# An mLSTM layer and a mixture of experts on one core: routing of units 16 to 19, the second expert's w2, the last logits and the q/k loads are moved or reshaped

## The chip, the cores and the metric

The kernel runs on one NeuronCore of a Trainium2 chip. The metric is the device time of one execution in microseconds. Engines are named as in the profile: PE (matmul), PEld (its weight loads), DVE (vector), ACT (scalar), POOL (GpSimd), SP (the engine that issues most DMAs).

## The reference

An mLSTM recurrence over 4 batches, 8 heads, 768 tokens with head width 40 gives x (3072 tokens of 320 numbers). A two-level mixture of experts works on x: 4 groups of 4 experts, a hidden width of 1024, the best group and in it the best expert for each token.

```python
m_new = np.maximum(f_gate[:, :, t] + m, i_gate[:, :, t])
f_stab = np.exp(f_gate[:, :, t] + m - m_new)
i_stab = np.exp(i_gate[:, :, t] - m_new)
C = f_stab[:, :, None, None] * C + i_stab[:, :, None, None] * np.einsum('bhd,bhe->bhde', vt, kt)
n = f_stab[:, :, None] * n + i_stab[:, :, None] * kt
denom = np.maximum(np.abs(nq), 1.0)
y[:, :, t] = o * h_tilde / denom
...
g_idx = np.argmax(x @ w_group, axis=1)
e_idx = np.argmax(x[mask_g] @ w_expert[g], axis=1)
h = np.maximum(xg[mask_e] @ w1[g, e], 0.0)
out[tok_idx] = combined[:, None] * (h @ w2[g, e])
```

`combined` is the product of the two softmax weights of the chosen group and expert.

## The kernel before, in words

**Attention.** The recurrence is computed in 6 chunks of 128 tokens. A chunk of one batch is a *unit*, u = 4 c + b, so there are 24. `unit(u)` writes one step of a software pipeline in which neighbours overlap: `scores` (`sp`, L204) of u, `norm1`, `rows`, `rows2` (x, L298) and `store` of u - 1, `mask` (POOL's AFFINE_SELECT, L158) of u + 1, `carried` (`it`, L229), `values` (`av`, L276), `state` (L248), `decay` (`aw` on PE, then four exponentials `ab` on ACT, L187) of u + 2, and `turn` (`tp`, `xT`) of u - 1. q and k lie transposed in a `qk` tile, the heads of r = 0 from partition 0, those of r = 1 from partition 64, 40 rows each; `load_qk` (L140) fills each half with its own DMA of 48 rows (8 of them padding). `store` writes x to DRAM (`x_d`).

**Routing.** For chunks 0 to 4, `logits_of(c)` multiplies the four `xT` tiles of a chunk with the gate weights, ACT copies the result to `lT` (L357), and `logits_back(c)` turns it back (L360) and appends `route` (L365) to `chores`. `route` is a chain of DVE steps (mx, df, eq, m, oh), ranks on PE (L399 to L408), and DVE again (cntf, pr, slf, slot). `go_on(n, slot)` hands out the next steps: "B" steps on DVE at the end of a unit, "A" the ranks on PE. `put_id` (L481) then writes the 128 token numbers of a unit into the table `itab` by an indirect DMA of POOL: four puts a chunk. The last chunk is routed as units 20 to 22 and unit 23 by `logits(u)` (`lg`, L342).

**Order.** Up to unit 21 the instructions stand in the order in which the code writes them; from unit 22 on a scheduler places them, apart from edges that `issue_after` adds.

**Experts.** At unit 14 `first_experts` picks the two experts with the most tokens so far. Their weights are loaded early, half a matrix at a time, by the list `early_loads`: one a unit in units 14 to 19 (w1 of the first, its w2, w1 of the second), the rest, the second's w2, at unit 22. `split_tasks` cuts them into high and low parts (ACT `w1h`, `w2h`, `wsk`; DVE `w1l`, `w2l`, L640). The first expert begins with 256 rows whose tokens are all of chunks 0 to 4: `load_ix` (L611) reads their numbers from `itab`, `load_x` (L578) gathers the rows in two `xg` tiles, `turn_tasks` turns them on PE (`tpm`, L306), and `expert` multiplies with w1 (`psh`, L747) and w2 (`po`). `busy(n)` are matmuls without a reader.

Two `issue_after` edges at the end of the main function (L1005 to L1007) tie the two `tpm` blocks: the first behind `lg` of unit 22, the second behind `tp` of unit 23.

## Time and profile before

| | us |
|---|---|
| three timed runs, median (lowest, highest) | 415.28 (415.12, 416.69) |
| the profiled execution | 414.25 |
| its span | 412.6 |
| PE busy in the span | 386.7 (94%) |
| DVE, ACT, POOL busy | 262.6, 213.7, 167.8 |

The profile is of one execution; all rows below belong to it. A timeline row gives the start from the beginning of the span, the busy time and, in brackets, the engine's idle time before it with what ended that.

### The profile page before, as it was taken

What the parts mean: (1) busy time and instruction counts of PE and PEld (TensorE: products, weight loads), DVE (VectorE), ACT (ScalarE), POOL (GpSimd) and SP (SyncE); (2) the same over time, 40 slices, a digit from 0 to 9 for tenths busy, and PEclk for the clock granted to TensorE, in tenths of its full rate; (3) what the DMA queues carried; (4) which work ended last, traced back from release to release, by engine and by line L of the source; (5) the groups of instructions that cost most, each with busy time, mean ns of one, the idle gap of its engine ahead of it and who ended that gap; (6) DMA issues with size and microseconds to landing.
All of it is one profiled execution on the core that took longest, in us unless ns stands there. A gap on an engine that the chain in (4) does not pass through costs nothing.

```text
span 412.6 us, 9857 instructions
## 1 busy us (share of the span) xinstructions
PE 386.7 (94%) x3665; PEld 361.5 (88%) x3665; DVE 262.6 (64%) x692; ACT 213.7 (52%) x541; POOL 167.8 (41%) x226
## 2 busy tenths in 40 slices
PE   8869999999998985599999999999999999999994
PEld 4769899998887874399999999999999999999994
DVE  5596876868789775385875664765745655433530
ACT  4754555555556611353855564755745645443520
POOL 3235576675664351345805234342032324322300
PEclk9998999999999988579999999999999999999999
DMA  7985789996899981147897557666753267877700
GB/s 201 243 267 151 221 103 222 268 211 136 237 260 240 230 234 42 41 152 239 277 408 250 165 195 256 240 224 185 290 220 136 65 244 258 295 290 262 251 17 11
DMA packets 29029, 84.97 MB, mean 206 GB/s; under 512 B 11831, under 2 KB 15790, under 8 KB 25396
## 3 DMA queue, kind: packets, MB, share of 16 engines
q1 hardware_dynamic: 23812, 67.63, 56.6%
q0 software_dynamic: 4944, 16.34, 11.6%
q8 instruction: 29, 0.48, 0.5%
q10 hardware_dynamic: 224, 0.35, 0.4%
q14 instruction: 20, 0.16, 0.2%
HBM read 74.55 MB, written 9.99 MB: 205 GB/s over the span
## 4 chain that ended last, share of the span: by engine, by line
PE 70%; DMA 12%; issue 9%; POOL 3%; DVE 3%; POOLq 1%; ACT 1%; SPq 0%; DVEq 0%
PE psh L747 14%; PE av L276 7%; PE po L769 6%; PE po L768 6%; PE po L770 6%; PE psh L715 6%; PE sp L204 4%; DMA w2s<-in_w_dram 3%; PE it L229 3%; PE tpm L306 3%; PE aw L177 2%; DMA itab<-tokid,slot 2%; PE it L248 2%; DMA nt<-in_nat_dram 2%; PE po L774 2%
## 5 line engine op out<-in xcount | busy, mean ns | idle before, releaser
L187 ACT ACTIVATE ab<-aw,bcol 128x128 f32<-128x128 f32 x192 | 54.5, 370 | 50.1 <-PE aw L177 49.7
L582 POOL DMA_INDIRECT out_dram<-y,ix x32 | 37.8, 1181 | 82.8 <-ACT y L780 68.8
L768 PE MATMUL po<-w2h,hh 128*128 128x320 f32 (+3 forms) x200 | 63.1, 316 | 0.0
L770 PE MATMUL po<-w2h,hh 128*128 128x320 f32 (+3 forms) x200 | 61.8, 309 | 0.0
L769 PE MATMUL po<-w2l,hh 128*128 128x320 f32 (+3 forms) x200 | 61.8, 309 | 0.0
L640 DVE TENSOR_TENSOR w2l<-w2s,w2h 128x640 fp32r<-128x640 f32 x64 | 50.6, 815 | 10.6 <-ACT w2h L638 10.6
L578 POOL DMA_INDIRECT xg<-x_d,ix x32 | 35.3, 1102 | 53.8 <-DMA ix<-itab 33.0
L276 PE MATMUL av<-nt,pt 128*128 128x128 f32 x384 | 50.1, 285 | 0.1
L276 PEld LDWEIGHTS av<-nt,pt 128*128 128x128 f32 x384 | 47.6, 201 | 0.9 <-DVE pt L209 0.3
L704 DVE SCALAR_TENSOR_TENSOR hh<-psh,hh 128x256 fp32r<-128x256 f32 (+4 forms) x108 | 36.0, 366 | 18.0 <-ACT hh L701 17.5
L701 ACT ACTIVATE hh<-psh 128x288 fp32r<-128x288 f32 (+8 forms) x68 | 30.1, 443 | 30.1 <-PE psh L747 15.4
L638 ACT CAST w2h<-w2s 128x640 fp32r<-128x640 f32 x64 | 43.2, 724 | 0.4 <-DMA w2s<-in_w_dram 0.4
L715 PE MATMUL psh<-xhl,w1s 128*128 128x144 f32 (+3 forms) x336 | 41.3, 283 | 0.0
L715 PEld LDWEIGHTS psh<-xhl,w1s 128*128 128x128 f32 x336 | 40.9, 191 | 0.1
L780 ACT ACTIVATE y<-po,xg 128x320 f32<-128x320 f32 (+3 forms) x25 | 13.2, 527 | 52.1 <-PE po L770 49.7
L747 PE MATMUL psh<-xhl,w1h 128*128 128x256 f32 (+5 forms) x224 | 38.6, 295 | 0.9 <-DVE xhl L683 0.5
L209 DVE TENSOR_TENSOR pt<-sp,ab 128x512 f32<-128x512 f32 x48 | 31.0, 685 | 10.2 <-PE sp L204 9.3
L769 PEld LDWEIGHTS po<-w2l,hh 128*128 128x128 f32 (+3 forms) x200 | 36.5, 183 | 0.0
L768 PEld LDWEIGHTS po<-w2h,hh 128*128 128x128 f32 (+3 forms) x200 | 36.5, 182 | 0.0
L770 PEld LDWEIGHTS po<-w2h,hh 128*128 128x128 f32 (+3 forms) x200 | 36.4, 182 | 0.0
L747 PEld LDWEIGHTS psh<-xhl,w1h 128*128 128x128 f32 x224 | 32.5, 196 | 1.5 <-DVE xhl L683 0.8
L204 PE MATMUL sp<-qk 40*128 40x128 f32 x384 | 29.5, 286 | 1.3 <-DVE pt L209 1.3
(193 smaller groups left out, 772.4 us busy)
## 6 DMA issues: line engine op xcount, KB each, us to landing
w1s<-in_w_dram SPq DMA_DIRECT2D x12, 1536.0 KB, 6.9
w2s<-in_w_dram SPq DMA_DIRECT2D x12, 1280.0 KB, 7.9
qk<-in_qkT_dram SPq DMA_DIRECT2D x48, 192.0 KB, 6.7
nt<-in_nat_dram SPq DMA_DIRECT2D x24, 324.0 KB, 6.3
x_d<-x SPq DMA_DIRECT2D x24, 192.0 KB, 7.1
sig<-in_og_dram SPq DMA_DIRECT2D x6, 640.0 KB, 7.1
w1s<-in_w_dram SPq DMA_DIRECT2D x4, 768.0 KB, 10.9
w1s<-in_w_dram POOLq DMA_DIRECT2D x2, 1536.0 KB, 7.1
```

Source lines behind the costliest of these rows:

```text
L187: rt["exp"] = nc.scalar.activation(st_[u]["ab"][:, r, j, :], aw[:, j, :], AF.Exp, bias=bcol[:, c, i:i + 1])
L204: mm(t["pm"][r][:, pr, :], qk[rs, 0, pr, :], qk[rs, 1, pr, :], start=True, stop=True)
L276: ins = mm(av[:, i:i + P], t["pm"][r][:, pr, :], nt[:, o:o + P], start=True, stop=True)
L582: return nc.gpsimd.indirect_dma_start(out=out, out_offset=bass.IndirectOffsetOnAxis(ap=idx, axis=0), in_=y, in_offset=None, bounds_check=N ...
L638: nc.scalar.copy(a, src[:, s])
L640: lows.append(lambda: nc.vector.tensor_tensor(o[rows], src[rows, s], a[rows].bitcast(F32), op=ALU.subtract))
L704: nc.vector.scalar_tensor_tensor(hh[:, f:f + per, dst], src[:, :, t], 0.0, hr.bitcast(F32)[:, :, t], op0=ALU.max, op1=ALU.subtract)
L715: ins = mm(ps[:, g * W:(g + 1) * W], w1s[:, s], xhl[:, k, :], start=(k == 0), stop=(k == 2))
L747: ins = mm(ps[:, g * W:(g + 1) * W], w[:, s], x, start=(n == 0), stop=(n == len(todo) - 1))
L768: mm(po[0:m], hh[:, f, t], w2h[:, s], start=st0, stop=False)
L769: mm(po[0:m], hh[:, f, t], w2l[:, s], start=False, stop=False)
L770: ins = mm(po[0:m], hh[:, f, tl], w2h[:, s], start=False, stop=sp0)
```

## The change

- `load_qk` is one DMA of 80 rows, into partitions 24 to 103 of the `qk` tile. r = 0 now contracts rows 0 to 63, the first 24 of which are zeros that POOL writes once; r = 1 contracts rows 64 to 103 as before. `kw` gets the same places, with POOL's zeros between.
- `logits_of(c)` stands ahead of the second `decay` of its unit, `logits_back(c)` at the end of the same unit (before: in the next unit).
- In unit 21, `route` of chunk 4 is written in the middle of the unit: four "B" steps ahead of `rows2`, the ranks, three "B" steps, and all four `put_id` there.
- The two halves of the second expert's w2 are issued by POOL instead of SP; POOL also loads that expert's number into a register for it.
- Both `tpm` blocks of the first expert are tied behind `lg` of unit 23.

```diff
+Z = 64 - D
+KS = 64 + D
-    kws = [ap_.tile([P, H * D + 24], F32, name=f"kw{i}") for i in range(2)]
+    kws = [ap_.tile([P, 4 * KS + Z], F32, name=f"kw{i}") for i in range(2)]
+    rows_of = slice(0, 64), slice(64, 64 + D)
@@ load_qk
-        for r in range(2):
-            nc.sync.dma_start(qk[64 * r:64 * r + QR], qkT[c, b, r])
+        nc.sync.dma_start(qk[Z:64 + D], qkT[c, b])
@@ scores, carried
-                rs = slice(64 * r, 64 * r + D)
+                rs = rows_of[r]
@@ first_experts
-            early_loads.extend(load_tasks(r, 2))
+            early_loads.extend(load_tasks(r, 2, None if r == 0 else [nc.sync, nc.gpsimd]))
@@ unit
         run(state2, u - 1)
+        if u == 21:
+            go_on(4, "B")
         run(rows2, u - 1)
...
         run(turn, u - 1)
-        if u % B == 1 and 1 < u < NU:
-            logits_back(u // B - 1)
         go_on(9, "A")
+        if u == 21:
+            go_on(3, "B")
+            for _ in range(B):
+                put_id()
...
         run(state, u)
+        if u % B == 0 and 0 < u < NU:
+            logits_of(u // B - 1)
         run(lambda v: decay(v, 1), u + 2)
...
         if u % B == 0 and 0 < u < NU:
-            logits_of(u // B - 1)
+            logits_back(u // B - 1)
@@ start
+        for t in qkp[0:2]:
+            nc.gpsimd.memset(t[0:Z], 0.0)
...
         for t in kws:
-            nc.gpsimd.memset(t[:, H * D:], 0.0)
+            nc.gpsimd.memset(t, 0.0)
+        for t in qkp[2:]:
+            nc.gpsimd.memset(t[0:Z], 0.0)
@@ behind the units
     turns = turn_tasks((0, 0), EARLY, xgs[0], ((ps_a, "aw"), (ps_s, "sp")))
-    for k in ("lg", NU - 2), ("tp", NU - 1):
-        with tc.issue_after(rt[k].ins), tc.high_priority():
-            do(turns, 1)
+    with tc.issue_after(rt["lg", NU - 1].ins), tc.high_priority():
+        do(turns)
```

The rest of the diff follows from the new rows: the slices of `keyw`, `state` and the arrangement of the input, and one argument more in `load_tasks` for the queue.

On DVE in unit 21 (xn and x are of unit 20, pt and num of unit 21, mx to oh route chunk 4), before:

```order
L292 SCALAR_TENSOR_TENSOR xn<-sig,av 128x320
L298 TENSOR_TENSOR x<-xn,den 128x2x4x40
L209 TENSOR_TENSOR pt<-sp,ab 128x512 x2
L236 TENSOR_TENSOR num<-it,eacol 128x328
L373 TENSOR_REDUCE mx<-lg 128x20
L375 TENSOR_TENSOR df<-lg,mx 128x80
L385 SCALAR_TENSOR_TENSOR eq<-df,cs 128x80
L388 TENSOR_REDUCE m_2482<-eq 128x20
L390 TENSOR_TENSOR oh_2484<-eq,m_2482 128x80
L394 TENSOR_TENSOR oh<-oh_2484 128x64
L640 TENSOR_TENSOR w2l<-w2s,w2h 128x640
```

and with the change:

```order
L293 SCALAR_TENSOR_TENSOR xn<-sig,av 128x320
L374 TENSOR_REDUCE mx<-lg 128x20
L376 TENSOR_TENSOR df<-lg,mx 128x80
L386 SCALAR_TENSOR_TENSOR eq<-df,cs 128x80
L389 TENSOR_REDUCE m_2408<-eq 128x20
L391 TENSOR_TENSOR oh_2410<-eq,m_2408 128x80
L395 TENSOR_TENSOR oh<-oh_2410 128x64
L299 TENSOR_TENSOR x<-xn,den 128x2x4x40
L210 TENSOR_TENSOR pt<-sp,ab 128x512 x2
L237 TENSOR_TENSOR num<-it,eacol 128x328
L413 COPY cntf<-lg 128x16
```

The six routing steps moved ahead of x, pt and num, and no w2l stands between them and cntf.

On POOL from the mask of unit 22 on (the first four `itab` are the puts of chunk 4, the next four those of the last chunk, `li` is the index of the first expert's late rows), before:

```order
L158 AFFINE_SELECT ab<-ab 128x1024 x2
L485 DMA itab<-tokid,slot 49280x1 x4
L611 ISA
L611 DMA ix<-itab 128x3x1
L578 DMA xg<-x_d,ix 128x392 x2
L485 DMA itab<-tokid,slot 49280x1 x4
L588 TENSOR_LOAD ewi
L596 ISA
L596 DMA w1s<-in_w_dram 128x3072
L578 DMA xg<-x_d,li 128x392
```

and with the change from the last put of chunk 4 on (the other three stand right ahead of it, behind the mask of unit 22):

```order
L486 DMA itab<-tokid,slot 49280x1
L485 MEMSET sep 1x1 x4
L159 AFFINE_SELECT ab<-ab 128x1024
L613 ISA
L613 DMA ix<-itab 128x3x1
L597 ISA
L597 DMA w2s<-in_w_dram 128x1280
L579 DMA xg<-x_d,ix 128x392 x2
L597 ISA
L597 DMA w2s<-in_w_dram 128x1280
L486 DMA itab<-tokid,slot 49280x1 x4
L579 DMA xg<-x_d,li 128x392
```

The mask of unit 23 now follows the puts, the two halves of w2s stand around the first gathers, and the third expert's w1s (3072 columns) left its place ahead of the gather by `li`.

On PE from the token transpose of unit 23 on, before:

```order
L306 MATMUL tp<-cs,x 128x128 x3
L306 MATMUL tpm<-cs,xg 128x128 x3
L124 LDWEIGHTS ones_b
L124 MATMUL busy<-ones_b 128x512
L124 LDWEIGHTS ones_b
L124 MATMUL busy<-ones_b 128x512
L342 MATMUL lg<-wc,xT 128x20 x3
```

and with the change:

```order
L307 MATMUL tp<-cs,x 128x128 x3
L126 LDWEIGHTS ones_b
L126 MATMUL busy<-ones_b 128x512
L126 LDWEIGHTS ones_b
L126 MATMUL busy<-ones_b 128x512
L126 LDWEIGHTS ones_b
L126 MATMUL busy<-ones_b 128x512
L343 MATMUL lg<-wc,xT 128x20 x3
L307 MATMUL tpm<-cs,xg 128x128 x3
```

The three logits passes of unit 23 (L342, now L343) moved ahead of the first tpm. Up to the second tpm follow four `busy` before, and three with the change.

## Rows read from the trace of the kernel before

**Rows 1.** The chain that ended last, 105 to 185 us: start, us, what.

```profile
145.93 0.70 POOL itab L485
...
150.93 9.97 issue
...
165.12 3.06 DMA xg<-x_d,ix
...
172.84 0.90 PE tpm L306 x3
...
175.37 9.58 PE psh L747 x63
```

**Rows 2.** Timeline of PE: start, us, engine, line, operation, out<-in, count, idle before and its releaser.

```profile
12.03 0.67 PE L248 MATMUL it<-nt,kw 128*64 128x41 f32 x16
...
131.27 0.39 PE L177 MATMUL aw<-Apc,sel_b 128*128 128x128 bf16 x4 [1.07 <-ACT ab L187]
131.58 1.16 PE L204 MATMUL sp<-qk 40*128 40x128 f32 x16
...
134.43 1.95 PE L276 MATMUL av<-nt,pt 128*128 128x128 f32 x16
...
147.17 1.61 PE L204 MATMUL sp<-qk 40*128 40x128 f32 x12 [1.28 <-DVE pt L209]
...
162.16 0.52 PE L306 MATMUL tp<-cs,x 128*128 128x128 f32 x3 [0.34 <-DVE ohs L424]
...
168.22 0.90 PE L306 MATMUL tpm<-cs,xg 128*128 128x128 f32 x3 [5.55 <-DMA xg<-x_d,ix]
```

**Rows 3.** Windows: us, then each engine's busy us (instructions), clock, DMA share, GB/s.

```profile
60.00:80.00 20.00, 20.00 (x295) 18.49 (x294) 14.76 (x46) 11.47 (x40) 14.26 (x22) 1.00 0.99 228
142.00:150.00 8.00, 6.27 (x73) 5.82 (x73) 7.97 (x32) 2.15 (x7) 4.35 (x5) 0.95 0.95 237
154.00:160.00 6.00, 5.47 (x50) 5.03 (x47) 3.19 (x12) 0.72 (x2) 0.00 (x0) 1.00 0.22 43
172.00:178.00 6.00, 5.01 (x23) 3.78 (x22) 4.86 (x26) 4.38 (x6) 0.96 (x1) 0.50 0.04 2
200.00:250.00 50.00, 50.00 (x366) 49.20 (x365) 35.29 (x83) 30.75 (x60) 18.14 (x18) 1.00 0.72 270
```

**Rows 4.** Timeline of DVE, units 20 to 23.

```profile
137.95 1.34 DVE L298 TENSOR_TENSOR x<-xn,den 128x320 f32<-128x320 f32 x1
...
140.81 0.23 DVE L373 TENSOR_REDUCE mx<-lg 128x20 f32<-128x80 f32 x1
...
142.31 0.82 DVE L640 TENSOR_TENSOR w2l<-w2s,w2h 128x640 fp32r<-128x640 f32 x1
...
145.50 0.16 DVE L419 CAST slot<-slf 128x4 int32<-128x4 f32 x1
...
161.53 0.48 DVE L298 TENSOR_TENSOR x<-xn,den 128x320 f32<-128x320 f32 x1
```

**Rows 5.** Timeline of SP's queue.

```profile
140.15 1.81 SPq L596 DMA_DIRECT2D w2s<-in_w_dram  x2
...
177.86 0.34 SPq L1026 DMA_DIRECT2D li<-itab  x1
```

**Rows 6.** Timeline of POOL, start-up and joint.

```profile
6.92 0.71 POOL L941 MEMSET Cflat<- 128x743 f32 x1
...
9.48 0.73 POOL L216 TENSOR_TENSOR kw<-nt,ab 128x320 f32<-128x320 f32 x1 [1.85 <-ACT ab L187]
...
175.13 0.96 POOL L485 DMA_INDIRECT itab<-tokid,slot  x1 [5.23 <-DVE slot L419]
...
180.00 0.57 POOL L596 DMA_DIRECT2D w1s<-in_w_dram  x1 [3.91 <-DVE eidr L552]
```

**Rows 7.** DMA issues: engine, count, KB each, median us to landing.

```profile
w1s<-in_w_dram POOLq DMA_DIRECT2D x2, 1536.0 KB, 7.1
```

**Rows 8.** Timeline of ACT.

```profile
126.74 1.27 ACT L155 ACTIVATE sig<-sig 128x1280 f32<-128x1280 f32 x1 [0.91 <-DMA sig<-in_og_dram]
```

More of the change, by code (lines that the diff above doesn't have):

```diff
@@ L33 @@
 D1 = D + 1
+Z = 64 - D
+KS = 64 + D
 HC = 4 * D1
 NQK = 4
-QR = 48
 C_ID, C_LT, C_TIE, C_E, C_P, C_CAP, C_FIRST, C_15E, C_BASE, C_SEL, C_END = 0, 128, 256, 260, 276, 277, 293, 309, 325, 341, 373
@@ L215, in keyw @@
             kw = t["kw"] = kws[u % 2]
-            nc.gpsimd.tensor_tensor(kw[:, 0:H * D].rearrange("p (j r d) -> p r j d", r=2, d=D),
+            nc.gpsimd.tensor_tensor(kw[:, 0:4 * KS].rearrange("p (j w) -> p j w", w=KS)[:, :, Z:KS].rearrange("p j (r d) -> p r j d", r=2),
                                     t["nt"][:, DM + H:].rearrange("p (j r d) -> p r j d", r=2, d=D),
@@ L226, in carried @@
                 for r in range(2):
-                    rs = slice(64 * r, 64 * r + D)
+                    rs = rows_of[r]
                     o = (b * 4 + pr) * D1
@@ L247, in state @@
                 pr, r0 = j // 2, 64 * (j % 2)
-                mm(t["it"][r0:r0 + 64, 1, HC + pr * D1:HC + (pr + 1) * D1], t["kw"][:, j * D:j * D + 64],
+                mm(t["it"][r0:r0 + 64, 1, HC + pr * D1:HC + (pr + 1) * D1], t["kw"][:, pr * KS + r0:pr * KS + r0 + 64],
                    nt[:, j * D1:(j + 1) * D1], start=True, stop=True)
@@ L591, in load_tasks, with one @@
     def load_tasks(r, n, q=None):
-        def one(t, name, src, w, k):
+        def one(t, name, src, w, k, q):
             if k == 0:
@@ L596, in one @@
             (q or nc.sync).dma_start(t[r][:, s], src[bass.ds(ereg[r], 1), :, s].rearrange("o p c -> (o p) c"))
-        return [lambda a=a, k=k: one(*a, k) for a in ((w1st, "w1s", w1, 3 * F), (w2st, "w2s", w2, NF * DM))
+        qs = q if isinstance(q, list) else [q, q]
+        return [lambda a=a, k=k, q=q: one(*a, k, q) for a, q in zip(((w1st, "w1s", w1, 3 * F), (w2st, "w2s", w2, NF * DM)), qs)
                 for k in range(n)]
@@ L1128, in tr @@
     def tr(a):
-        a = a.reshape(B, H // 2, 2, NCH, P, D).transpose(3, 0, 2, 5, 1, 4)
-        return np.concatenate([a, np.zeros_like(a[:, :, :, :QR - D])], axis=3)
-    qkT = c(np.stack([tr(k), tr(q)], axis=4))
+        return a.reshape(B, H // 2, 2, NCH, P, D).transpose(3, 0, 2, 5, 1, 4)
+    qkT = c(np.stack([tr(k), tr(q)], axis=4).reshape(NCH, B, 2 * D, 2, H // 2, P))
     def rows(a):
```

## The prediction

> **What bounds the kernel now.** The profiled execution took 414.25 us (span 412.6), 1.03 below the median of the three timed runs, 415.28; the sum below is made against the profiled one and 1.03 is added at the end. I read the windows first. From 60 to 80 us TensorE (PE) is busy 20.00 of 20 us, and from 200 to 250 us 50.00 of 50 [rows 3]: attention and experts are both PE-bound, and in them only PE work counts. Between them lies a joint: from 154 to 160 PE still does 5.47 of 6 us, but from 172 to 178 it runs at a granted clock of 0.50, the 1.2 GHz level [rows 3]. So I read the chain of waits there. In it the joint starts with the token numbers of chunk 4 (units 16 to 19): four puts on POOL from 145.93 to 150.93; then 9.97 us of "issue", in which POOL stands at the load of `ix` until the puts have landed; at 160.9 the index load, then two gathers, the first of which lands at 165.12 + 3.06 = 168.18; then PE turns the tokens (the second block at 172.84), and the first expert's `psh` starts at 175.37 [rows 1]. The timeline of PE shows the same from its side: it idles 5.55 us at 168.22 for the gather, although the last transpose of attention, tp(23), stands at 162.16 [rows 2]. The logits of unit 23 need only tp(23), but stand behind the first token transpose in PE's order. Everything after `psh` is PE-bound, so what the joint loses the kernel loses.
>
> **80-row loads.** 64 KB less per unit and 24 SP issues less. While PE is full [rows 3] this is worth nothing. It is worth something where PE waits for data: at 131.27 PE idles 1.07 for ACT's exponentials [rows 2], and ACT had stood 0.91 for the load of `sig` [rows 8]. With about four units' 64 KB out of the way ahead of `sig` and the half matrix behind it, 256 KB at the 228 GB/s of a full stretch [rows 3] are 1.1 us. Bounds 0 and -1.07; I take -0.8, as the half matrix may still be a little late. At the start POOL gets two memsets of 1024 columns and two wider ones of `kw` ahead of `Cflat`: by the 0.71 us for 743 columns [rows 6] about 2.5 us more, so POOL is done at 10.1 instead of 7.6 (two more memsets stand before all else, where POOL waits for its first data). `keyw` of unit 0 goes from 9.48 to about 10.1 [rows 6] and ends at 10.9; its reader, state(0), starts on PE at 12.03 [rows 2]. That is the cover, so I take 0; without it PE would lose what is over 12.03.
>
> The two matmuls of r=0 now contract 64 rows instead of 40, the first 24 of them zeros. Sixteen passes of 40 rows take 1.16 us, sixteen of 128 rows 1.95 [rows 2], so pairs of 40-row passes overlap; no row here shows 64. Bounds: 0, or 0.79 for each of 24 + 20 bursts, 35 us. I take 0, since the two halves still lie in separate 64-row halves of the array, as before. TensorEngine Tiling (Array Packing), a page of the Trainium skill, section When to Use Tiling, gives twofold row tiling up to a contraction of 64; by it the term is 0, by the 128-row bound alone it would be 35, and no run so far shows which.
>
> **Logits earlier.** `logits_back` now stands right behind `logits_of` and one `decay`; PE may wait for ACT's copy of `lT` between them. The matmul itself is only moved. Five times 0 to 0.2 us; I take +0.3 in all.
>
> **Units 16 to 19 routed within unit 21.** Now mx to oh (six DVE steps) stand from 140.81 to 142.31, behind x(20), pt(21) and num; then two slices of w2l (0.82 for the first) are mixed among the steps that lead to `slot` at 145.50 [rows 4]. After the change mx follows xn directly, that is where x(20) stands now, 137.95; the six steps take 1.6, so x(20) comes at 139.5 and pt(21), num behind it end at about 141.5 (they end at 140.9 now); cntf to slot need some 0.2 each and no w2l stands among them: slot at 142.3 to 143.3. With 0.8 from above taken off the later value, the first put is at 142.6 against 145.93, and with the pace of now (145.93 to 150.93) the last ends at 147.6. tp(20) on PE waits for x(20) by up to 0.8 us; PE idles 1.28 at 147.17 for pt(22) on DVE anyway [rows 2], and DVE has 1.6 us of w2l less ahead of that, so I take 0 for it. Queued behind the four puts on POOL is only the mask of unit 23, at about 148.8; pt(23) comes later.
>
> **Second matrix behind the first gathers.** Two 640 KB halves leave SP, where they are issued at 140.15 [rows 5], ahead of the puts. When do the puts land? Lower bound: the put at 175.13, on idle rings, had its reader issued at 177.86 [rows 5, 6], 2.7 later: 147.6 + 2.7 = 150.3. Upper bound: as late as now, 10.0: 157.6. I take 152.5, nearer the lower end, because 1.28 MB that now lie ahead of them come behind them. From the end of that wait to the gathered rows it is 168.18 - 160.9 = 7.3 [rows 1]. In the same POOL queue the first half matrix now goes ahead of the two gathers: 640 KB at the 270 GB/s of rows 3 are 2.4 us, hidden partly by the wait for `ix`: 0 to 2.4, I take 0.9. So the rows are there at 152.5 + 7.3 + 0.9 = 160.7. Trainium Kernel Development and Optimization, the first page of the Trainium skill, section Key Constraints, speaks against this part: queues of SP, ACT and POOL share 16 DMA engines, and issuing elsewhere saves issue time only. By it the move alone gives nothing and only its later place in time does; that is the first rival's ground.
>
> **Last logits first.** x(23) ends on DVE at 161.53 + 0.48 = 162.0 [rows 4]. DVE is busy 7.97 of 8 us from 142 to 150 [rows 3] and sets this end; 1.6 us of w2l leave that stretch, and 0.8 comes from the loads: 159.6. Bounds: 162.0 if neither reaches it, 158 if the 0.9 that x(20) takes over the 0.48 of x(23), and the 0.6 left of slot's delay, go too [rows 4]. Transpose, copy and lg(23) take 0.5 + 0.5 + 0.9: 161.5. So PE is free for the first token transpose at about 161.5 and the rows are there at 160.7: the two ends meet, and attention binds by a little. From the first to the second transpose is 4.62 now, with logits and `busy` between [rows 1, 2]; then three `busy` alone, about 2.2 at the low clock and 1.3 at the high one, and 2.53 (1.7) from there to `psh`: 4.7 or 3.0. I take 3.8, as less idle time precedes it.
>
> **Sum.** `psh` at 161.5 + 3.8 + 0.3 = 165.6 instead of 175.37 [rows 1]: -9.8. The experts keep their length if their data comes: the first expert's rows on SP and POOL move with `psh`; the third expert's w1 (issued at 180.00 now, landing in 7.1 [rows 6, 7]) stands behind four gathers more, so at about 180.0 - 9.8 + 5 = 175, there by 185. The second half of the second expert's w2 goes out behind the gathers at about 160 and is wanted only after the first expert. 414.25 - 9.8 = 404.45, plus 1.03: **405.5 us**.
>
> **Rivals.**
> - *The puts land as late as now* (10.0 us behind the last one; the loads before them are what delays them, not the half matrices). For: several transfers of that stretch are still issued ahead. Against: DMA is busy only 0.22 from 154 to 160 [rows 3]. Gathers at 157.6 + 7.3 = 164.9, `psh` 4.7 later at 169.6: 409.5; with the half matrix fully ahead of the gathers 411.9. Chance 0.14.
> - *Attention's end binds, without a gain on DVE*: x(23) stays at 162.0, lg(23) ends at 163.9, `psh` at 168.6: 408.5. Chance 0.10.
> - *The clock holds and all gaps close*: transposes at 160, `psh` at 163: 402.9. Chance 0.08.
> - *No gain arrives*: the third expert's w1, moved behind the gathers of tokens for the second, comes so late that PE waits the gain away: about 415. It would need to land 10 us later than I work out. Chance 0.03.
> - *Slower*: 64-row passes no longer overlap with their 40-row partner. It decides in each `sp` and `it` burst from the first unit on: 16 passes at over 1.16 us, up to 1.95 [rows 2], 44 times; PE is full there, so all 35 us count: 440. It is slower in the end from 0.27 us per burst on. Against: the other half of the rows is unchanged. Chance 0.04.
>
> **Numbers.** The forecast has 0.61: 405.5, alone 403 to 408. The range 401.0 to 411.5 takes in it and the first three rivals but for their outer ends. A measurement here can tell about 0.5%, 2.1 us. Faster: 0.61 + 0.14 + 0.10 + 0.08 = 0.93; same 0.03; slower 0.04.
>
> **What would show it.** Sixteen `sp` passes still in 1.16 us; no wait of ACT for `sig` at about 126; the first of four puts near 142.6, with one mask operation of POOL ahead of them and one behind; a wait of POOL for their landing of 5 us instead of 10; the gathers landing near 161, with lg(23) ahead of tpm on PE and an idle time of under 1 us there; `psh` near 165.6, and the same length from `psh` to the end of the span (237.2). Wrong it would be if `psh` came later than 170, if the time after `psh` grew, or if `sp` bursts were longer.

## The result, and the profile after

| | before | after |
|---|---|---|
| median of the runs on one chip | 415.28 us (413.83 to 416.86, 11 runs) | 411.12 us (407.99 to 415.75, 11 runs) |
| after / before | | 0.9887 [0.9853, 0.9921] |
| profiled execution: time, span | 414.25, 412.6 | 411.12, 409.5 |
| xn of unit 20 on DVE (attention) | 137.48 | 140.59 |
| first `psh` matmul of the first expert | 174.31 | 171.01 |
| first `psh` to the end of the span | 238.3 | 238.5 |

The change is faster by 1.13%, some 4.7 us; the forecast was 9.8 us. The ratio leaves out the two slow runs of the change (414.36 and 415.75 us), which the medians contain. The three last lines of the table, of one execution each, say where to look. Up to xn(20) the change has *lost* 3.11 us. From there to the first `psh` it takes 30.42 instead of 36.83 us, 6.4 less. Behind `psh` nothing moved in total. (The forecast counted `psh` from the 175.37 of the chain [rows 1]; the first of its matmuls stands on PE at 174.31, which is used from here on.)

The joint, in the timeline of PE after the change, answering to [rows 2] (start, us, engine, line, operation, out<-in, count, idle before it and its releaser):

```profile
133.56 1.16 PE L205 MATMUL sp<-qk 64*128 64x128 f32 x16
...
135.87 1.16 PE L230 MATMUL it<-Cflat,qk 64*128 64x128 f32 x16 [1.15 <-DVE Cflat L264]
...
150.63 0.71 PE L277 MATMUL av<-nt,pt 128*128 128x128 f32 x4 [1.35 <-DVE pt L210]
...
163.94 0.18 PE L400 MATMUL lg<-oh,lt_b 128*128 128x48 bf16 x1 [2.07 <-DVE oh L395]
...
164.55 0.52 PE L307 MATMUL tp<-cs,x 128*128 128x128 f32 x3 [0.34 <-DVE ohs L425]
164.91 1.47 PE L126 MATMUL busy<-ones_b 128*128 128x512 bf16 x3
166.18 1.30 PE L343 MATMUL lg<-wc,xT 128*128 128x20 f32 x6
167.32 0.88 PE L307 MATMUL tpm<-cs,xg 128*128 128x128 f32 x3
...
171.01 1.67 PE L749 MATMUL psh<-xhl,w1h 128*128 128x256 f32 x4 [0.45 <-ACT xhl L684]
...
197.38 0.37 PE L770 MATMUL po<-w2h,hh 128*80 128x320 f32 x1 [0.93 <-ACT hh L703]
```

The wait of 5.55 us for the gather [rows 2] is gone: tpm at 167.32 stands right behind lg(23) and waits for nothing. So it is not the rows that set the time now but the end of attention: tp(23) at 164.55, three `busy`, lg(23). `sp` over 64 rows takes 1.16 us, as over 40. Three waits are new: 1.15 for DVE at 135.87, where 1.07 for ACT stood before [rows 2], 0.54 for x(20) at 143.85 (which the forecast put at up to 0.8 and took as 0), and 0.93 at 197.38.

POOL after the change, answering to [rows 6]:

```profile
146.28 0.97 POOL L486 DMA_INDIRECT itab<-tokid,slot  x1 [3.30 <-DVE off L530]
...
148.82 1.52 POOL L486 DMA_INDIRECT itab<-tokid,slot  x1 [0.22 <-issue]
...
150.65 1.16 POOL L486 DMA_INDIRECT itab<-tokid,slot  x1 [0.21 <-issue]
...
158.40 0.83 POOL L613 DMA_DIRECT2D ix<-itab  x1 [4.74 <-DMA itab<-tokid,slot]
...
181.09 0.99 POOL L579 DMA_INDIRECT xg<-x_d,li  x1 [7.11 <-DVE cntr L562]
...
186.52 0.59 POOL L597 DMA_DIRECT2D w1s<-in_w_dram  x1
```

The puts begin 0.35 us later than before, not 3.3 earlier. Counted from xn(20) they do come earlier, by 2.76 us (5.69 behind it instead of 8.45), so the earlier routing works and it is attention that is late. From the start of the last put to the load of `ix` it is 7.75 us (158.40 - 150.65) instead of 11.18 (160.91 - 149.73). The third expert's w1 goes out at 186.52 instead of 180.00 [rows 6].

Windows after the change, answering to [rows 3] (us, then busy us of PE, PEld, DVE, ACT, POOL with their instructions, granted clock of TensorE, DMA share, GB/s). The first window had a clock of 0.83 before:

```profile
26.00:36.00 10.00, 7.03 (x59) 6.33 (x57) 8.04 (x18) 3.66 (x11) 4.33 (x5) 0.66 0.31 88
...
154.00:160.00 6.00, 5.99 (x63) 5.64 (x62) 3.44 (x9) 0.72 (x2) 1.41 (x2) 0.93 0.12 36
...
166.00:172.00 6.00, 5.41 (x23) 3.63 (x23) 3.46 (x23) 3.06 (x6) 2.43 (x4) 0.50 0.40 124
172.00:178.00 6.00, 6.00 (x39) 6.00 (x39) 4.65 (x14) 4.54 (x7) 1.98 (x1) 0.72 0.05 4
200.00:250.00 50.00, 50.00 (x365) 49.17 (x364) 35.26 (x82) 30.20 (x59) 17.37 (x18) 1.00 0.73 274
```

The experts are full as before. The joint's last 6 us still run at 0.50, the 1.2 GHz level, and near 30 us, behind a wait of PE of 2.83 us at 29.47, the low level now lasts longer.

### The profile page after: what moved, and what is told of

Its sections match the earlier page's. It is cut to its first block, busy times and chain, and to the rows that moved or that the text cites. A ratio compares the mean times of both kernels' runs of the same rounds, so it can differ in the third digit from the quotient of the medians.

```text
span 409.5 us, 9797 instructions
## 1 busy us (share of the span) xinstructions
PE 387.6 (95%) x3665; PEld 361.1 (88%) x3665; DVE 263.9 (64%) x692; ACT 213.4 (52%) x541; POOL 173.9 (42%) x232
## 4 chain that ended last, share of the span: by engine, by line
PE 69%; DMA 10%; issue 9%; DVE 5%; POOL 3%; ACT 2%; POOLq 1%; SPq 0%; ACTq 0%; DVEq 0%
PE psh L749 12%; PE av L277 9%; PE psh L717 6%; PE po L770 6%; PE po L772 6%; PE po L771 6%; PE sp L205 4%; PE it L230 3%; DMA w2s<-in_w_dram 3%; DMA x_d<-x 3%; PE it L249 2%; PE po L776 2%; PE aw L178 2%; PE tpm L307 2%; PE po L775 2%
## 5 line engine op out<-in xcount | busy, mean ns | idle before, releaser
L583 POOL DMA_INDIRECT out_dram<-y,ix x32 | 36.9, 1154 | 78.6 <-ACT y L782 71.3
L486 POOL DMA_INDIRECT itab<-tokid,slot x24 | 25.9, 1080 | 15.3 <-DVE slot L420 4.3
```

What stands on the lines that cost most here:

```text
L583: return nc.gpsimd.indirect_dma_start(out=out, out_offset=bass.IndirectOffsetOnAxis(ap=idx, axis=0), in_=y, in_offset=None, bounds_check=N ...
```

## Experiments

Questions: what did attention lose, what part brings the gain, and what bounds the joint once it is shorter? Each ratio is against the kernel before on the same chip; its median was 411.7 to 412.2 on three of the chips and 414.6 to 415.3 on the others, so times of different chips are not compared, and ratios of different chips only with care. The experiments leave no part of the computation out; fillers are matmuls that nobody reads.

### One part undone or alone

**Logits of chunks 0 to 3 back in their old place**

```diff
         run(turn, u - 1)
+        if u % B == 1 and 1 < u < 20:
+            logits_back(u // B - 1)
...
-        if u % B == 0 and 0 < u < NU:
-            logits_of(u // B - 1)
+        if u == 20:
+            logits_of(4)
```

> The changed kernel with the logits of chunks 0 to 3 where they stood before (logits_of behind the second decay, logits_back in the next unit behind turn); chunk 4 stays early, which its routing in unit 21 needs. In the changed kernel's trace xn of unit 20 stands at 140.59, 3.11 us later than before. Theory A (logits_back on PE waits for lT, and costs in each chunk): of the 3.11 about 1.1 to 1.4 go, in steps of 0.27 to 0.56 at units 5, 9, 13 and 17; xn(20) near 139.3, the time 1 to 1.4 us under the changed kernel's, so 409.7 to 410.1 at a median of 411.1. Theory B (the loss comes from the 80-row loads and POOL's order in the first units, or from the clock): under 0.4 us moves, no step at units 9, 13, 17.

Measured: 407.99 us, 0.9876 [0.9841, 0.9911]; xn(20) at 139.26 in the profile. The time can't be told from the change's own, but the profile can: 1.33 of the 3.11 us are back. How five moved matmuls cost that is seen at unit 9 in the timeline of PE. After the change:

```profile
66.78 0.40 PE L178 MATMUL aw<-Apc,sel_b 128*128 128x128 bf16 x4
67.23 0.33 PE L361 MATMUL lg<-cs,lT 128*128 128x128 f32 x1
67.49 1.16 PE L205 MATMUL sp<-qk 64*128 64x128 f32 x16
```

and in this experiment:

```profile
65.57 0.40 PE L178 MATMUL aw<-Apc,sel_b 128*128 128x128 bf16 x4
65.89 0.86 PE L356 MATMUL lg<-xT,wc 128*32 128x128 f32 x24
...
69.24 0.27 PE L361 MATMUL lg<-cs,lT 128*128 128x128 f32 x1
69.35 1.95 PE L277 MATMUL av<-nt,pt 128*128 128x128 f32 x16
```

A step of xn at a unit is by how much more it is late against before than at the unit ahead. In the old place the next matmul starts 0.11 us behind the logits' one. In the new place the step from `aw` to `sp` is 0.71 us, where `aw` to its follower is 0.32 without it: 0.39 - 0.11 = 0.28 us, and 0.26 is what xn(9) steps by. No idle time is listed, since the ends of matmuls are modelled; only the starts show it. xn steps by 0.56, 0.26, 0.28 and 0.38 at units 5, 9, 13 and 17.

**The change with the two 48-row loads of before**

```diff
-        nc.sync.dma_start(qk[Z:64 + D], qkT[c, b])
+        for r in range(2):
+            nc.sync.dma_start(qk[64 * r:64 * r + QR], qkT[c, b, r])
...
```

> The changed kernel with two 48-row DMAs per unit as before; all else as changed. Theory B (80-row loads cost attention 1.5 us or more: more work of POOL at the start, later first puts): xn(20) comes by 1.5 to 2 us earlier, the time falls to about 409.5. Theory A (only logits_back and the clock cost there, loads are worth 0 to 0.3 us while PE is full): xn(20) stays within 0.4 of 140.6 and the time within 0.5 of 411.1; the forecast's own term (0.8 us saved by them) would make it 411.9.

Measured: 412.41 us, 1.0005 [0.9981, 1.003]: without the new loads the whole gain is gone. The two profiles are only 1.2 us apart (span 410.7), and ACT waits for `sig` in neither. xn(20) comes at 142.22, 1.63 later than with the change. The window at the 1.15 us wait shows why, first of this experiment, then of the change:

```profile
134.00:140.00 6.00, 4.84 (x45) 4.43 (x44) 3.46 (x10) 2.60 (x10) 3.85 (x6) 0.72 1.04 193
```

```profile
134.00:140.00 6.00, 4.85 (x76) 4.42 (x73) 3.89 (x11) 2.57 (x10) 3.85 (x6) 1.00 1.06 205
```

PE is busy as long in both, but does 45 instructions in place of 76, at a granted clock of 0.72. Over its runs the mean clock was 0.965 to 0.973; over those of the change 0.970 to 0.982.

**The 80-row loads alone**

```diff
-            nc.sync.dma_start(qk[64 * r:64 * r + QR], qkT[c, b, r])
+        nc.sync.dma_start(qk[Z:64 + D], qkT[c, b])
...
```

> The kernel before with the 80-row loads alone (one DMA per unit, zeros by POOL, 64-row contraction). The forecast's term: -0.8 us, ratio 0.998. Theory B (the loads carry the change: without them, e2 was no faster than before, 1.0005, against 0.9887): ratio 0.987 to 0.991. Theory C (e2 lost its gain to half-clock stretches at 44 to 47 and 136 to 139, which e3, with the new loads, shows as well): ratio within 0.997 to 1.003, and its half-clock time decides where in that.

Measured: 411.95 us, 0.9986 [0.9965, 1.0006]: by themselves the loads give about 0.6 us, which can't be told from nothing. With the joint of before, unchanged, `ix` was loaded 8.02 us behind the start of the last put (150.72 to 158.74), not 11.18.

**The moved logits alone**

```diff
-        if u % B == 1 and 1 < u < NU:
-            logits_back(u // B - 1)
...
+        if u % B == 0 and 0 < u < NU:
+            logits_of(u // B - 1)
```

> The kernel before with only the logits moved (logits_of ahead of the second decay, logits_back at the end of the same unit). Theory A: PE loses 0.27 to 0.56 at each of five chunks in attention: xn(20) at 138.8 to 139.2 instead of 137.48; joint unchanged, so the time is 1.3 to 1.7 us longer, 416.6 to 417. Theory B: xn(20) within 0.4 of 137.48, time within 0.5 of 415.3.

Measured: 415.89 us, 1.0094 [1.006, 1.0129], slower by 3.9 us. The steps of 0.26 to 0.38 are there at units 9, 13 and 17; at unit 5 it is 3.56. The windows there, of before and of this experiment:

```profile
40.00:51.00 11.00, 10.40 (x162) 9.40 (x155) 8.63 (x26) 6.06 (x24) 6.19 (x10) 1.00 0.71 204
```

```profile
40.00:51.00 11.00, 10.39 (x92) 9.25 (x89) 5.75 (x17) 3.80 (x14) 3.69 (x6) 0.69 0.52 143
```

PE is equally busy, at 0.69 instead of 1.00: the clock fell behind a wait of 0.61 us at 42.96, which at 1.00 stood before as well (0.60 at 42.52). Behind `psh` this profile also has a wait of 3.48 us for the gather by `li` (at 189.52), which the profile of before has not; how much of the 3.9 us each of the two makes is not separated.

**Routing, second matrix and order of the joint alone, old loads, logits of chunk 4 early**

```diff
+        if u == 21:
+            go_on(4, "B")
...
-            early_loads.extend(load_tasks(r, 2))
+            early_loads.extend(load_tasks(r, 2, None if r == 0 else [nc.sync, nc.gpsimd]))
...
-    for k in ("lg", NU - 2), ("tp", NU - 1):
-        with tc.issue_after(rt[k].ins), tc.high_priority():
-            do(turns, 1)
+    with tc.issue_after(rt["lg", NU - 1].ins), tc.high_priority():
+        do(turns)
```

> The kernel before with the joint's parts alone: chunk 4's logits early, its routing in unit 21, w2 of the second expert on POOL, both tpm behind lg(23); old loads, and the logits of chunks 0 to 3 where they were. The forecast's terms for these: -9.0 us, ratio 0.978. The changed kernel's trace (psh 7.5 us earlier than attention's shift explains, 1.3 lost behind it): -5 to -6.2, ratio 0.985 to 0.988. Theory C with new half-clock stretches from SP's 48-row loads, as in e2: ratio 0.991 to 1.0, with half-clock stretches ahead of 140 us that the kernel before has not.

Measured: 410.04 us, 0.9928 [0.99, 0.9956], against the 0.978 of the forecast's terms. With the logits of chunks 0 to 3 moved as well, this is the kernel with the two 48-row loads above, at 1.0005: with the old loads these logits cost 3.2 us on top of it and 3.9 by themselves. With the new loads it is 0.9887 with them and 0.9876 without, which can't be told apart.

**Only the order of the last logits** (the last five lines of that diff alone)

```diff
-    for k in ("lg", NU - 2), ("tp", NU - 1):
-        with tc.issue_after(rt[k].ins), tc.high_priority():
-            do(turns, 1)
+    with tc.issue_after(rt["lg", NU - 1].ins), tc.high_priority():
+        do(turns)
```

> The kernel before with both tpm blocks tied behind lg(23), and nothing else; POOL's order then also puts the gather by li ahead of the third expert's w1. The gathers still land at about 168, so tpm stays there; from it to psh 2 us less than before (lg(23) done ahead). Forecast's view: psh 1.5 to 2.5 us earlier, ratio 0.994 to 0.997. Theory E: up to 1 of it is given back where PE waits for the third expert's w1, ratio 0.997 to 1.0.

Measured: 410.68 us, 0.9901 [0.9876, 0.9926]: this edit alone brings as much as the whole change. On POOL the scheduler then also puts the gather by `li` (176.15) ahead of the third expert's w1 (182.04). The timeline of PE:

```profile
163.91 1.31 PE L342 MATMUL lg<-wc,xT 128*128 128x20 f32 x6
165.05 0.88 PE L306 MATMUL tpm<-cs,xg 128*128 128x128 f32 x3
167.27 0.90 PE L306 MATMUL tpm<-cs,xg 128*128 128x128 f32 x3
168.74 1.67 PE L747 MATMUL psh<-xhl,w1h 128*128 128x256 f32 x4 [0.45 <-ACT xhl L682]
...
195.04 0.38 PE L768 MATMUL po<-w2h,hh 128*80 128x320 f32 x1 [1.14 <-ACT hh L701]
```

lg(23) no longer waits for the gather, and from tpm to `psh` it is 3.7 us as in the change (forecast 3.8). The puts are issued in their old place (145.13 to 148.94 us), and still the rows are there when tpm wants them: from the start of the last put to `ix` it was 6.74 us. This kernel has the old loads and attention of before, and yet ACT doesn't wait for `sig`, and PE's wait of 1.07 is replaced by one for DVE:

```profile
132.57 1.16 PE L229 MATMUL it<-Cflat,qk 40*128 40x128 f32 x16 [1.16 <-DVE Cflat L263]
```

**Only the routing in unit 21** (with the logits of chunk 4 early)

```diff
+        if u == 21:
+            go_on(3, "B")
+            for _ in range(B):
+                put_id()
...
```

> The kernel before with chunk 4's logits early and its routing and puts in unit 21, nothing else (w2 of the second expert on SP, old order of tpm). Forecast's view: puts 2.5 to 3.3 us earlier, gathers and psh with them, ratio 0.992 to 0.994. If attention's end or a half-clock stretch takes it: psh under 1 us earlier, ratio 0.998 or more.

Measured: 413.56 us, 0.9986 [0.9964, 1.0008]: nothing that can be told. In its profile xn(20) comes 1.52 us later than before, behind a stretch at the low clock from 133 us on (0.83 in the window from 130 to 140), and PE still waits 0.90 for the gather and 1.86 behind `psh`, at 199.10. Together with the order the earlier routing has not been seen to pay either: the version above with routing, second matrix and order has 0.9928, the order alone 0.9901, on two chips.

**Second matrix back on SP** (in the kernel with fillers in attention, below)

```diff
-            early_loads.extend(load_tasks(r, 2, None if r == 0 else [nc.sync, nc.gpsimd]))
+            early_loads.extend(load_tasks(r, 2))
```

> f1_fill_att with the second expert's w2 halves issued by SP again, ahead of the puts. The forecast's reason for this part (the halves ahead delay the puts' landing): the load of ix comes about 10 us behind the last put instead of 5.3, the first tpm waits for its rows until about 166 instead of 163.1, ratio 0.993 to 0.995. The first rival (the landing is late anyway) or attention's end as the bound: tpm stays at 163 to 163.5, ratio 0.986 to 0.988.

Measured: 406.72 us, 0.9878 [0.9855, 0.99], against 0.9866 [0.9837, 0.9894] with the matrix on POOL. The load of `ix` starts 1.6 us later (155.56 for 153.98) and PE waits 0.79 for the rows, but behind `psh` the wait for w1 (1.14 with the matrix on POOL) is gone, and the times, on two chips, can't be told apart.

### The clock

**Fillers at the waits of attention** (on the first experiment)

```diff
+        for _ in range({2: 14, 20: 3}.get(u, 0)):
+            mm(tp, ones_b, bc(ones_b.unsqueeze(1), (P, 3, P)), start=True, stop=True)
...
+        busy(4 if u == 20 else 0)
...
+        for _ in range(6 if n == 4 else 0):
+            mm(tp[:, 3 * w:4 * w], ones_b, ones_b, start=True, stop=True)
```

> e1_lgback_old with matmuls without a reader put into PE's four gaps of attention: 14 ahead of tp(2), 6 ahead of the ends matmul of the second gate sums, 4 ahead of `it` of unit 20, 3 ahead of tp(20). Nothing else moves. Theory C (short PE gaps are followed by stretches at half clock, and these took what the change gained in attention: 6.8 us at half clock before 60 us in the changed kernel's profile against 3.4 before, and in two of the later runs another 3.4 at 136 to 139): no half-clock stretch is left ahead of 140 us, xn(20) comes 2.5 to 3.5 us earlier than e1's 139.26, and the time falls by as much, to a ratio of 0.979 to 0.982 against e1's 0.988. Theory D (the gaps themselves are the price, the clock is an accompaniment): the fillers only occupy the gaps, xn(20) within 0.5 us of e1's, ratio 0.987 to 0.989.

Measured: 406.66 us, 0.9866 [0.9837, 0.9894]; xn(20) at 137.45, against 139.26 without the fillers, as early as before the change. The ratio can't be told from the 0.9876 without them, measured on another chip, and misses the 0.979 to 0.982 expected; what xn(20) gains is seen in the profile only. The window that stood at 0.66:

```profile
26.00:36.00 10.00, 8.80 (x100) 6.96 (x97) 9.62 (x21) 4.57 (x15) 5.37 (x7) 1.00 0.37 116
```

**The same fillers on the kernel before**

```diff
+        for _ in range({2: 14, 20: 3}.get(u, 0)):
+            mm(tp, ones_b, bc(ones_b.unsqueeze(1), (P, 3, P)), start=True, stop=True)
...
```

> The kernel before with f1's fillers in attention. Its profile has 3.4 us at half clock ahead of 140 us, behind the gap at 29.6. Theory C: that stretch goes, 1.6 to 1.7 us less, ratio 0.995 to 0.997, the joint stays as it is. If f1's gain over the changed kernel were all the fillers' own, the ratio would be the lower, 0.990.

Measured: 410.29 us, 0.9959 [0.9938, 0.998], as expected: the fillers are worth 1.7 us by themselves. `ix` was loaded 7.06 us behind the last put.

**Fillers in the joint too**

```diff
+        for _ in range(5 if u == 22 else 0):
+            mm(av, ones_b, bc(ones_b.unsqueeze(1), (P, 4, P)), start=True, stop=True)
...
+            with tc.issue_after(rt["lg", u].ins):
+                rt["fill"] = busy(8)
```

> f1_fill_att with fillers in the joint too: 5 ahead of av(22), 8 behind the logits of unit 22, with the ranks and tp(23) tied behind them. Theory C: the joint runs at full clock up to psh (e1 has 9.5 us of busy time at half clock from 128 to 200 us, so 4 to 5 us less), the first tpm stands right behind lg(23), psh at about 160 to 162, ratio 0.968 to 0.973. Theory D: the fillers take PE time that was free, psh is no earlier than in f1, ratio as f1 or 0.5 us worse for eight fillers ahead of the ranks.

Measured: 409.49 us, 0.9901 [0.9865, 0.9936]. (Here and in all later versions with the eight fillers the logits of unit 22 are also written ahead of tp(23), so that the fillers can stand between.) The five fillers ahead of av(22) cost more than the wait that they fill (xn(22) 2.5 us later), and behind `psh` PE waited 3.07 us for the third expert's w1.

### The third expert's first matrix

**w1 ahead of the late gathers, in the change**

```diff
+    with tc.high_priority():
+        load_w1(2, nc.gpsimd)
     for r in range(NEARLY):
         xgs[r, 1] = load_x(LATE, late_ix[r])
...
-    load_w1(2, nc.gpsimd)
```

> The changed kernel with the third expert's w1 issued by POOL ahead of the gather by li, as its order was before. In the changed kernel it is issued at 186.52, behind a gather that waits until 181.09, and ACT waits 1.31 and PE 0.93 for it. Theory A (this lateness costs what the time from psh to the end grew by, 238.49 against 237.23): the stretch from psh to the end falls back to about 237.3, the time by 0.9 to 1.3 to about 410. Theory B (the growth is the clock or the transfers' load, not the order): the wait goes but the stretch stays within 0.3 of 238.5.

Measured: 408.65 us (406.51 to 413.88), 0.9892 [0.9853, 0.9931]; from `psh` to the end 237.2 instead of 238.5, so the wait of 0.93 is gone from the profile, but the time can't be told from the change's.

**Fillers without those ahead of av(22), w1 first**

```diff
+                rt["fill"] = busy(8)
...
+    with tc.high_priority():
+        load_w1(2, nc.gpsimd)
```

> f1_fill_att with eight matmuls without a reader behind the logits of unit 22 (ranks and tp(23) behind them; none ahead of av(22), where f2's cost 2.5 us) and the third expert's w1 issued ahead of the gather by li, as in e3. Theory C with the next bound named (once psh is early, PE waits in the first po of the late rows for the third expert's w1: 0.93 in the changed kernel, 1.14 in f1, 3.07 in f2): psh at about 165, no such wait, 236 us from psh to the end as in f1 or less, ratio 0.973 to 0.977. Theory D (neither matters): ratio as f1, 0.987.

Measured: 407.55 us, 0.9876 [0.985, 0.9902]. `psh` comes at 163.70, 3.1 us earlier than with attention's fillers alone, and all of it is lost again: now the late gathers wait behind w1. The timeline of PE:

```profile
180.90 0.90 PE L308 MATMUL tpm<-cs,xg 128*128 128x128 f32 x3 [3.38 <-DMA xg<-x_d,li]
```

**The same with the change's place for the logits**

```diff
-        if u % B == 1 and 1 < u < 20:
-            logits_back(u // B - 1)
...
```

> g1_fill_w1 with the logits of chunks 0 to 3 where the changed kernel has them. Theory A (their place costs PE 0.27 a chunk by itself, more at the first): xn(20) 0.8 to 1.3 us later than in g1, ratio 0.002 to 0.004 above g1's. Theory C alone (their cost was the half-clock stretch they set off behind unit 4): no half-clock stretch there with the fillers, ratio within 0.002 of g1's.

Measured: 407.9 us, 0.989 [0.986, 0.992]; xn(20) 1.58 us later than in the one before, in the profile; the times overlap.

**w1 between the late gathers and those of the second expert** (on the fillers)

```diff
+        for r in range(NEARLY):
+            xgs[r, 1] = load_x(LATE, late_ix[r])
         load_w1(2, nc.gpsimd)
```

> g1_fill_w1 with the third expert's w1 between the gather by li and the three gathers of the second expert, instead of ahead of all. Theory E (one POOL queue and one set of rings serve the late rows and the third expert's w1; whichever goes last is waited for once psh is early: w1 in f1, 1.14, the late rows in g1, 3.38): in between neither is late, no idle time of PE over 0.6 between psh and 200 us, 236 us from psh to the end, ratio 0.974 to 0.979. Theory F (behind psh the transfers as a whole are the bound): a wait of 2 us or more stays somewhere, ratio 0.985 to 0.988.

Measured: 407.27 us (406.19 to 407.92), **0.9823 [0.98, 0.9847]**: the lowest ratio of all, 7.3 us under before; the intervals of three others (0.9858, 0.9866 and 0.9876) still overlap with it. The clock no longer falls in the joint (windows, then the waits that are left, in the timeline of PE):

```profile
150.00:170.00 20.00, 17.79 (x156) 14.65 (x155) 15.67 (x67) 9.03 (x17) 9.05 (x10) 1.00 0.40 108
...
180.00:200.00 20.00, 17.51 (x131) 16.73 (x130) 12.66 (x31) 12.28 (x30) 12.57 (x14) 1.00 0.98 381
```

```profile
164.41 0.38 PE L761 MATMUL psh<-xhl,w1h 128*128 128x256 f32 x1 [0.20 <-issue]
...
179.31 0.55 PE L308 MATMUL tpm<-cs,xg 128*128 128x128 f32 x3 [1.28 <-DMA xg<-x_d,li]
187.26 0.55 PE L308 MATMUL tpm<-cs,xg 128*128 128x128 f32 x3 [0.51 <-DMA xg<-x_d,ix]
192.41 0.37 PE L782 MATMUL po<-w2h,hh 128*80 128x320 f32 x1 [1.97 <-ACT hh L715]
```

3.8 us of the time won ahead of `psh` are lost in three waits, two of them in a stretch in which the DMA engines are busy 0.98 of the time.

**The same order without fillers, in the change**

```diff
+    with tc.high_priority():
+        for r in range(NEARLY):
+            xgs[r, 1] = load_x(LATE, late_ix[r])
+        load_w1(2, nc.gpsimd)
...
```

> The changed kernel with the third expert's w1 between the gather by li and the gathers of the second expert; no fillers. Theory E: no wait of ACT and PE for that w1, 237.2 instead of 238.5 from psh to the end, ratio 0.003 under the changed kernel's 0.9887, 0.985 to 0.987; its spread over runs stays as wide, as the half-clock stretches stay. Otherwise ratio 0.988 to 0.990.

Measured: 412.62 us, 0.9943 [0.9923, 0.9962]: worse than the change's 0.9887, as far as ratios of two chips can be compared, and the wait at the third expert's w1 is 1.83 us. By itself the order in the queue does not make the version above fast.

**w1 behind all gathers, with fillers**

```diff
-        load_w1(2, nc.gpsimd)
     xgs[1] = load_x(CAPS[1], ix_of(1))
+    load_w1(2, nc.gpsimd)
```

> h1_best with the third expert's w1 behind all four gathers again, as in the changed kernel. Theory E: PE waits 1 to 1.5 us longer for that w1 than in h1 (1.97), nothing else, ratio 0.984 to 0.987. Theory F (the transfers of 176 to 196 us as a whole are the bound, 0.96 of the DMA engines from 180 to 200 in f1; the order only moves the wait): ratio 0.981 to 0.984, as h1.

Measured: 408.47 us, 0.9858 [0.9812, 0.9904]; one wait of 3.10 us for w1 and one of 1.35 for the late gather. Wherever w1 stands in these three versions, 3.4 to 4.5 us are waited.

**Order of the last logits with fillers, nothing else**

```diff
+        for _ in range({2: 14}.get(u, 0)):
+            mm(tp, ones_b, bc(ones_b.unsqueeze(1), (P, 3, P)), start=True, stop=True)
...
+                rt["fill"] = busy(8)
```

> h2_turns_only (of the change, the order of the last logits alone) with the fillers of the start (14 ahead of tp(2), 6 ahead of the ends matmul) and the eight behind the logits of unit 22. If the change's other parts are worth what h1 (0.9823) has over h2 (0.9901) beside the clock: ratio 0.986 or more, psh at 167 or later, for the puts and x(23) are as late as before. If the clock was all that parted them: psh at 165.5 to 166.5, no half-clock stretch but at 149 to 153, ratio 0.981 to 0.984.

Measured: 412.03 us, 0.993 [0.9903, 0.9956]: no better than the order alone. In its profile the clock fell behind a wait of 0.86 us at 130.41, where this version has no filler (0.66 in the window from 130 to 140), and xn(20) came 2.4 us later than with the order alone; and PE waited 3.13 us for w1. The cause of the wait at 130.41 is that of the wait of 1.07 in [rows 2]: ACT stands for the load of `sig` again, with the old loads. ACT, then PE:

```profile
126.02 1.27 ACT L156 ACTIVATE sig<-sig 128x1280 f32<-128x1280 f32 x1 [0.82 <-DMA sig<-in_og_dram]
```

```profile
130.41 0.39 PE L178 MATMUL aw<-Apc,sel_b 128*128 128x128 bf16 x4 [0.86 <-ACT ab L188]
```

Over its runs the mean clock was 0.973 to 0.984, with the order alone 0.967 to 0.976: a higher clock, and no shorter time.

## Why the prediction was right in its sign and wrong in its size and most of its terms

**The step that failed.** "`psh` at 161.5 + 3.8 + 0.3 = 165.6 instead of 175.37 [rows 1]: -9.8." It came at 171.01, 3.3 us earlier than the 174.31 of the same matmul before, and later than the 170 that the forecast itself had named as a sign of being wrong. The end of attention was put too early: lg(23) was to be done at 161.5, and tpm stands behind it at 167.32. The 6.5 us that are missing are 3.6 of attention up to xn(20), 0.9 on x(23), 1.0 of `busy` and 1.06 of counting (175.37 is the second row of `psh`, not the first); each is treated below. Three of the four parts that were to bring the gain bring nothing that can be told by themselves (loads, routing, second matrix); the order of the last logits brings it.

**Right.** The wait for the gathers goes; lg(23) stands ahead of tpm; `sp` over 64 rows takes 1.16 us as over 40, and the pace of xn from unit 10 to 12 is that of before, so the slower rival (440 us) falls and the rule of TensorEngine Tiling (Array Packing), section When to Use Tiling, in the Trainium skill holds here; the length from `psh` to the end stays within 0.2 us in the two profiles. The sign was right.

**Luck.** From tpm to `psh` it is 3.7 us and the forecast had 3.8, but by other terms: it took the middle of 4.7 at the low clock, counted to 175.37, and 3.0 at the high one. The stretch ran at 0.50 throughout, where its own way gives 4.7; counted to the first `psh` that is 3.6. And the range (401.0 to 411.5) held the result near its upper end, which had been set for puts that land late, not for an attention that loses time.

**"Logits earlier ... +0.3 in all": mis-sized.** The steps of xn at units 5, 9, 13 and 17 sum to 1.48 us, and undoing them gives 1.33. The bound of 0.2 each left out the round trip through ACT's copy: PE has nothing to put between `logits_of` and `logits_back` but one `decay`.

**No term for the clock in attention.** The forecast carried the clock only in the joint. The low level after the wait at 29.47 lasted longer than before, 6.0 instead of 3.2 us of PE's busy time ahead of 60 us (summed over windows of 1 us): 2.7 us more at half the rate is some 1.3 us. With fillers there this is gone. xn's own steps put 1.03 on this stretch (units 3 and 4), 1.48 on the logits, 0.48 on unit 7 and 0.25 on unit 16; less 0.15 by which the change is ahead at unit 2, that is 3.09 of the 3.11. The step at unit 7 stands in all twelve profiles with the 80-row loads (0.11 to 0.53; alone 0.38) and is under 0.1 in the seven other experiments; that at unit 16 stands in the twelve with the second matrix on POOL and in none of the other seven. So both moves cost something where PE is full, which the forecast put at nothing; why is not shown.

**"80-row loads: -0.8": a wait that comes and goes.** After the change ACT no longer waits for `sig`, and PE's wait of 1.07 us went with it. But so it is in the experiment that only reorders the last logits, with the old loads. Of the eight profiles with the old loads two show the wait (before, and the last experiment above with 0.82), of the twelve with the new ones none. So the loads may make it rarer, which two of eight do not show, but they removed nothing that stood in every run. Nor did its going pay, since DVE was next: with the order alone xn(20) comes at 137.45 without the wait and at 137.48 before with it. In the timeline of DVE after the change it works without a break up to `Cflat`, and PE waits 1.15 us:

```profile
132.10 1.22 DVE L642 TENSOR_TENSOR wsk<-w1s,wsk 64x1024 fp32r<-64x1024 f32 x1
133.35 0.82 DVE L642 TENSOR_TENSOR w2l<-w2s,w2h 128x640 fp32r<-128x640 f32 x1
...
135.50 0.32 DVE L264 TENSOR_TENSOR Cflat<-Cflat,it 128x164 f32<-128x164 f32 x1
```

What is late next was asked in the joint and not here. Instead of 0.5 us early (-0.8 + 0.3) attention's end came 3.1 late: 3.6 us.

**"x(23) at 159.6, lg(23) done at 161.5".** x(23) comes only 0.7 us earlier relative to xn(20), not 1.6, and the three `busy` ahead of lg(23) take 1.47 us at the low clock. They stood in the order and were not counted, some 1.0 us. So attention's end binds, later than even the second rival had it (x(23) at 162.0; it ended at 164.4). Attention's 3.6, 0.9 on x(23) and 1.0 for `busy` make up the 5.4 us by which `psh` (171.01) came later than the forecast's 165.6.

**"As late as now, 10.0": the number of one profile.** Seven other kernels that leave the second matrix on SP loaded `ix` 6.7 to 8.1 us behind the start of the last put; twelve with it on POOL, the change among them, 6.0 to 7.8. Only the profile of before shows 11.2; the kernel before was profiled once, so whether its other executions have it, or its chip makes it, is not known. The wait that the forecast set out to shorten is 3.1 to 4.4 us shorter in the seven profiles with the matrix still on SP, and attention's end covers it as soon as the order is mended. The 6.4 us won between xn(20) and `psh` hold some of this: with the joint as before, the loads alone take 33.6 us for it and the fillers alone 32.7, not 36.8. The Trainium skill (Trainium Kernel Development and Optimization, section Key Constraints) says that all these queues run on the same 16 DMA engines and that issuing from several of them saves issue time only; 0.9878 with the matrix on SP and 0.9866 on POOL agree as to the time, though with it on POOL the puts landed 1.6 us sooner.

**"No gain arrives ... 0.03": it came true in part.** w1 of the third expert went out 6.5 us later and PE waited 0.93 us for it. It cost little only because the gain ahead of it was small: where `psh` came at 163.7 to 166.9, PE waited 1.1 to 4.5 us behind it in six of the seven profiles; the seventh, without a wait, is the one with the second matrix on SP.

**What is shown and what is not.** Shown: the order of the last logits alone gives about the whole gain (0.9901 against 0.9887); the routing alone and the loads alone give nothing that can be told; the moved logits alone, with the old loads, lose 3.9 us. The parts don't add up: without the new loads the change gains nothing (1.0005). The profiles point to the clock, but the same code had a stretch at the low level in one execution and not in another: the version with w1 first differs from the change only behind attention, yet its xn(20) came at 142.34. What decides whether the clock falls at a short wait is open, and with it why the change without the new loads lost all its gain. The shares of the 3.11 us are read from one profile of each kernel. That the DMA engines as a whole bound the stretch from 180 to 200 us is argued from their 0.98 and from the three places of w1, which all end in waits, and not shown. Against it speaks the version with fillers in attention and the second matrix on SP, where they are busy 0.96 and PE never waits (psh there at 166.92):

```profile
180.00:200.00 20.00, 20.00 (x153) 19.95 (x152) 14.35 (x38) 12.99 (x32) 11.75 (x14) 1.00 0.96 355
```

The version with the lowest ratio was not tried with the second matrix on SP, nor with w1 in another queue.

## What to carry to other kernels

Before you forecast the removal of a wait, see in a second profile whether it stands there too: of the two that this forecast rested on, one was 3 us longer than in any other profile and the other came and went without an edit. Look first for an instruction that stands behind a wait it doesn't need: reordering the last logits on PE gave what the whole change gave. And a short idle time on PE can cost a second time through the clock behind it, so a matmul that is moved "for nothing" is to be priced with the stretch that follows, and a filler at that place can pay by itself (0.9959 here).

## What the runs showed of the hardware

- The granted clock fell to the 1.2 GHz level after waits of PE as short as 0.6 us (at 42 to 44 us) and 1.15 us (at 135), and in other executions of the same code did not. Independent matmuls in the waits of attention kept it at 1.00 up to 140 us in the eight profiles with all of these fillers.
- One kernel's time went with its mean clock in two kernels: the change's runs at 0.970 to 0.976 took 410.4 to 414.0 us, those at 0.981 and 0.982 408.0 to 409.6; the version with w1 first took 411.5 at 0.970 and 406.5 at 0.983. It is no rule: the order of the last logits with fillers (the last experiment) took 410.0 us at 0.981 and 412.8 at 0.984. A profile taken at one end of such a spread shows 5 us that an edit neither made nor saved.
- From an indirect put of four to its reader's start it took 6.0 to 8.1 us among other transfers, once 11.2.
